# Sharing one buffer between the cosine's argument and g, a fourth P buffer, normalisation per tile, unchecked registers and a new order in a sparse-attention and cosine-MLP kernel

## The chip, the cores and the metric

One Trainium2 chip, one of its cores. The metric is the device time of one execution in microseconds (us); the smaller the better. Engines are TensorE (PE; its weight loads are shown as PEld), VectorE (DVE), ScalarE (ACT), GpSimd (POOL) and SyncE (SP, which only issues DMAs here). A q behind an engine's name means its sequencer.

## What is computed

Block-sparse attention over 4 batches of 8 heads, 768 positions and 64 dimensions, then a feed-forward layer whose nonlinearity is h cos(h):

```python
mask = |block_i - block_j| <= 1, or block_i or block_j first or last   # blocks of 32
mask |= three sampled blocks for each query block
attn = softmax(where(mask, q @ k.T / 8, -1e9))
x = (attn @ v)            # (4, 8, 768, 64) -> (3072, 512)
h = x @ w_in              # w_in is 512 x 2048, float64
out = (h * cos(h)) @ w_out   # w_out is 2048 x 512, float64
```

## The kernel before

**Tiles.** The 3072 rows are 24 query tiles of 128 rows, six to a batch. Five of the six are sparse: each row of queries sees 11 blocks of keys (352 columns). The sixth holds the first and the last blocks and is dense (768 columns, as 2 x 384). A sparse tile is worked in four units of two heads, a dense one in eight units of one head. Two tiles make one feed-forward m of 256 rows; there are 12 of them. A feed-forward has four pieces p of 512 hidden columns.

**Precision.** Operands are split into a high and a low half of float16; a product is high x high, high x low and low x high. V is stored as [high | low], 128 columns a head.

**A unit.** Scores into the PSUM tile `sp` (one slot), bias add with maximum into `P` (`mx`), a small op for the exponent's bias (`nb`), exp (`ex`, its row sums go to `sums`), high half into `ring` (`ph`, ScalarE), low half (`pl`, VectorE), a DMA transpose of `ring` to `PT`, then the products with V into the PSUM tile `xp` (`pv`). `P`, `ring` and `PT` have three slots each.

**Values.** In `sparse_values` (L1641, L1653) and `dense_values` (L1666) a wide unit multiplies the high half of P by [V high | V low], 128 columns, and the low half by V high, 64 columns, so that `xp` has 128 columns a head for four heads, one PSUM bank. Sparse tiles before number 6 are `thin`: three products of 64 columns that add up in the same 64 columns. A sparse unit has first its quarter products (96 x 32 weights at four row positions), then its full ones.

**Normalisation** comes after two sparse or four dense units, twice a tile (`normalize`): offset of the sums (`rs`, L1679 or L1682), reciprocal (`rr`, L1686), multiply by it (`no`, L1689), for wide tiles an add of the two 64-column halves (`xa`, L1691), cast to float16 (`xh`, L1693) and the rest (`xl`, L1696), all on VectorE. The DMA transpose to `xT` follows once a tile is complete.

**A feed-forward piece.** TensorE makes 48 "up" matmuls (L1831) into `ph`; ScalarE evacuates them to `hs` (L1840, two slots) in two halves; VectorE rounds (`round_a`, `round_b`, L1845 and L1848) into `kt` (one slot); ScalarE takes the sine in place (L1851, another table than exp's); VectorE multiplies back into `hs` (L1855); ScalarE and VectorE write the high and low halves of `g` (L1861 and L1864, four slots); TensorE makes 24 "down" matmuls (L1873).

**Start.** The first k and v are loaded and scaled; a scale comes from a Gram product on TensorE (L1316), a reduction (L1319) and a spread. 32 weight blocks arrive as float64, are converted by integer operations on VectorE (L1742 to L1746), scaled and split. Raw blocks lie in weight tiles that are not yet in use and, for the last eight, in `g` slots. The third v load lies in the `kt` slot. Sampled indices are loaded into registers (`load_regs`, L1204) on VectorE and ScalarE, eight and four for each of five tile positions, with a check of each value against its bounds.

**Order.** No engine's order is written out. Each operation has an engine, a cost, a position in time (from `PARAMS` and a nudge by its name from `NUDGES`), its operands and its slots. `Plan.run` is a list scheduler that goes through all engines at once, takes on each the runnable operation of least position, and hands out slots in the sequence of the first operations' positions. What results is a fixed program order for each engine; on the chip the engines run in order and wait for one another by semaphores. The lines that put the rounding where it is:

```python
op("DVE", 0.602, pos + ae(p, 2) + pr["KT"], lambda hs=hs, kt=kt: e.round_a(hs.t, kt.t), r=[hs], w=[kt], name=f"ka{m}_{p}")
op("ACT", 0.947, pos + ae(p, 5) + pr["GH"], lambda hs=hs, g=g: e.g_hi(hs.t, g.t), r=[hs], w=[(g, 0)], name=f"gh{m}_{p}")
```

with KT = -33.478 and GH = 9.373.

Of the kernel before, what the change touches and what calls it, by code (L numbers as in the profile page):

```python
# [13 lines left out]
F32 = mybir.dt.float32  # L14
I32 = mybir.dt.int32
AF = mybir.ActivationFunctionType
ALU = mybir.AluOpType
# [3 lines left out]
P = 128  # L21
BLK = 32
# [13 lines left out]
    VLEAD=6.432, EVAC=-1.668, KT=-33.478, SN=-2.897, GM=-10.655, GH=9.373, GL=8.736, TSTICK=31.117,  # L36
# [6 lines left out]
    RG=[0.0, -3.58, 20.03, 0.0, -2.44], RA=[2.07, 9.34, 0.26, 1.6, 9.28], PV3=[1, 1, 1, 1, 1, 1],  # L43
# [4 lines left out]
    QLP=[0, 0, 0, 0, 0, 0], XLP=[0, 0, 0, 0, 0, 0],  # L48
# [9 lines left out]
    idx=-7.77, sx=31.62, regs=-0.29, regs0=4.25, regs0_0=0.33, regs1=15.75, regs1_0=-22.8, regs2=48.02, regs2_0=5.02, regs0_1=-18.23, const=25.72,  # L58
    kload=-0.12, kload0=3.07, kload0_0=-4.36, ksq=1.03, ksq0=0.62, ksq0_0=-19.66, kload0_1=-3.8, ksq0_1=4.89, kload0_2=-15.73, ksq0_2=-6.31,
    kred=-16.28, kred0=11.53, kall=-0.88, kall0=-3.2, ksc=-8.35, ksc0=-5.35, regs3=3.42, regs3_0=9.11, regs4=-9.54, regs4_0=0.87, regs2_1=-7.41,  # L60
    regs3_1=5.19, regs4_1=1.21, vload=1.17, vload0=-0.48, vload0_0=1.69, vsq=1.1, vsq0=-8.19, vsq0_0=3.52, vload0_1=-1.23, vsq0_1=1.21,
    vload0_2=28.21, vsq0_2=-20.52, vred=17.47, vall=0.47, vall0=-18.65, vsc=7.33, vsc0=0.49, ql=-1.59, ql0=-2.36, qsq=0.12, qsq0=-0.63, qsc=-0.5,
    qsc0=-28.56, qu=-1.19, qu0=-3.51, qnu=3.74, qnu0=-8.16, qhi=1.19, qhi0=-7.92, qlo=0.44, qlo0=11.7, uT=-0.15, uT0=14.1, up=-12.11, up0=-4.28,
    khi=4.28, khi0=8.38, klo=4.06, klo0=6.12, kT=2.7, kT0=-7.25, kT0_2=0.33, kp=-2.83, kp0=3.56, kp0_2=-1.28, kT0_3=-12.7, kp0_3=10.63, kT0_4=3.23,
    kp0_4=3.3, kT0_5=1.89, kp0_5=5.32, vhi=0.77, vhi0=-1.22, vhi0_0=-11.14, vlo=-20.9, vlo0=-1.23, vlo0_0=5.58, vst=13.41, vst0=1.18, vst0_0=-16.89,
    vhi0_1=0.55, vlo0_1=-4.78, vhi0_2=-11.3, vlo0_2=-10.17, vst0_2=10.69, vhi0_3=14.56, vlo0_3=10.79, vst0_3=-18.61, vhi0_4=0.71, vlo0_4=23.48,
    vst0_4=7.73, vhi0_5=3.61, vlo0_5=-14.89, vst0_5=1.21, vg=-0.55, vg0=34.29, vg0_0=34.43, vg0_1=6.76, vg0_2=-25.78, vi=8.02, vi0=-3.57, vi0_0=7.48,
    vi0_1=-3, vi0_2=8.01, vi0_3=-37.84, wgd=-1.11, wgd0=-17.02, wga=0.34, wga0=13.21, wl=-6.98, wl0=1.07, wc=0.23, wc0=-0.77, wc0_0=-7.39,
    wc0_2=-6.83, wsq=-9.45, wsq0=13.98, wl1=1.26, wc1=11.01, wc1_0=-3, wc1_1=4.52, wc1_2=-3.38, wsq1=5.06, wl2=-11.17, wl3=4.27, wc3=-1.76,
# [1882 lines left out]
```

## Time and profile before

| | |
|---|---|
| three runs | 868.88, 874.35, 879.92 us, median 874.35 |
| profiled execution | 885.61 us, its span 883.8 us |
| PE busy, its mean granted clock | 739.3 us (84%), 0.94 |
| DVE busy | 681.3 us (77%) |
| ACT busy | 628.2 us (71%) |
| POOL busy | 99.4 us (11%) |
| DMA | 146.45 MB, mean 166 GB/s |

The times are of separate executions; the profile is of another one, and its durations fit its own time. Busy time of an engine leaves out its register and semaphore work. An engine that is busy 80% of a span may still not be what ends last, which is why the stretches and the chain of waits are read beside it.

### The profile page before, as it was taken

The page shows a single profiled execution, that of the slowest core. Times are in us where ns is not written, and L with a number is a line of the kernel's source. Part 1 is how long each engine was busy: PE and PEld are TensorE (multiplying, and loading weights), DVE is VectorE, ACT ScalarE, POOL GpSimd, SP SyncE. Part 2 cuts the span into 40 slices and gives each one's busy share as a digit, 9 for nine tenths or more (in the row PEclk, how much of TensorE's full clock was granted, in tenths as well). Part 3 has the DMA queues.
Part 4 walks back from the last instruction along what each step waited for, and adds up shares of the span by engine and source line. Part 5 has one row for each costly group of instructions (what it writes and reads, how often), then busy time and mean ns, then how long its engine had stood idle before and what let it go on. Part 6 is the DMA issues. An engine that isn't in the chain of part 4 may idle for free.

```text
span 883.8 us, 21557 instructions
## 1 busy us (share of the span) xinstructions
PE 739.3 (84%) x8360; PEld 506.6 (57%) x8360; DVE 681.3 (77%) x1813; ACT 628.2 (71%) x1181; POOL 99.4 (11%) x128
## 2 busy tenths in 40 slices
PE   2445687769698898999999888989999789899997
PEld 2334564457456556758566457657675458467583
DVE  1868999998966887878867975989868768866652
ACT  1655765889766987767867976779669847959442
POOL 5021220000021021200022021200040111000000
PEclk9997688869989999999999889999999789999999
DMA  8799894587886999794778998794888997963400
GB/s 253 239 245 209 214 234 133 130 173 149 168 226 149 172 217 176 145 212 91 139 230 168 188 190 186 150 216 84 187 198 148 180 168 151 215 107 76 82 7 24
DMA packets 316118, 146.45 MB, mean 166 GB/s; under 512 B 266480, under 2 KB 291184, under 8 KB 316016
## 3 DMA queue, kind: packets, MB, share of 16 engines
q1 hardware_dynamic: 310896, 129.35, 70.8%
q0 software_dynamic: 5120, 15.73, 7.8%
q8 instruction: 65, 1.06, 0.5%
q14 instruction: 37, 0.30, 0.1%
HBM read 68.23 MB, written 12.58 MB: 91 GB/s over the span
## 4 chain that ended last, share of the span: by engine, by line
PE 36%; DVE 25%; DMA 17%; ACT 10%; issue 6%; DVEq 2%; another core or an unknown queue 2%; SPq 1%; ACTq 0%
PE po L1873 14%; PE ph L1831 14%; DMA PT<-ring 7%; DVE P L1580 4%; DVE ring L1616 2%; DMA W<-kn 2%; DMA stage<-in_k_dram 2%; ACT P L1602 2%; PE xp L1653 2%; DVE hs L1855 2%; DVEq L1204 2%; PE sp L1564 2%; DVE kt L1848 2%; DMA w<-in_moe_w_out_dram 2%
## 5 line engine op out<-in xcount | busy, mean ns | idle before, releaser
L1873 PE MATMUL po<-w,g 128*128 128x512 f16 x1152 | 285.3, 397 | 12.5 <-DVE kn L1889 5.8
L1831 PE MATMUL ph<-xT,w 128*128 128x256 f16 x2304 | 266.0, 274 | 11.7 <-DMA xT<-n 4.3
L1831 PEld LDWEIGHTS <-w 128*128 128x128 f16 x2304 | 224.3, 98 | 48.6 <-issue 11.3
L1873 PEld LDWEIGHTS <-g 128*128 128x128 f16 x1152 | 110.2, 101 | 139.6 <-issue 29.4
L1602 ACT ACTIVATE P<-P,sm 128x352 f32<-128x352 f32 (+1 forms) x224 | 152.1, 680 | 51.4 <-DVE sm L1597 45.4
L1519 POOL DMA_INDIRECT V<-scr,gidx x80 | 88.1, 1101 | 646.6 <-PE xp L1641 288.5
L1616 DVE TENSOR_TENSOR ring<-P,ring 128x704 f16<-128x704 f32 (+1 forms) x112 | 100.3, 905 | 16.5 <-ACT ring L1612 16.2
L1580 DVE CUSTOM_DVE_ANT_1 P<-sp,bias 128x352 f32<-128x352 f32 x160 | 78.5, 518 | 29.8 <-PE sp L1553 15.6
L1840 ACT ACTIVATE hs<-ph,sm 128x512 f32<-128x512 f32 x96 | 64.1, 678 | 44.6 <-PE ph L1831 30.5
L1612 ACT CAST ring<-P 128x704 f16<-128x704 f32 (+1 forms) x112 | 86.6, 785 | 10.4 <-DMA PT<-ring 9.6
L1547 PE MATMUL sp<-W,U 128*128 128x192 f16 x320 | 54.8, 272 | 39.8 <-DVE sm L1580 31.5
L1855 DVE SCALAR_TENSOR_TENSOR hs<-hs,sm,kt 128x1024 f32<-128x1024 f32 x48 | 61.5, 1280 | 18.8 <-ACT kt L1851 18.5
L1851 ACT ACTIVATE kt<-kt,sm 128x1024 f32<-128x1024 f32 x48 | 55.1, 1147 | 22.2 <-DVE kt L1848 22.0
L1861 ACT ACTIVATE g<-hs 128x1024 f16<-128x1024 f32 x48 | 50.1, 1049 | 27.2 <-DVE hs L1855 27.2
L1864 DVE TENSOR_TENSOR g<-hs,g 128x1024 f16<-128x1024 f32 x48 | 58.3, 1219 | 6.3 <-ACT g L1861 5.7
L1548 PEld LDWEIGHTS <-U 128*128 128x128 f16 x320 | 33.7, 105 | 48.4 <-issue 44.9
L1848 DVE SCALAR_TENSOR_TENSOR kt<-kt,hs 128x1024 f32<-128x1024 f32 x48 | 58.6, 1220 | 0.4
L1845 DVE TENSOR_SCALAR kt<-hs 128x1024 f32<-128x1024 f32 x48 | 33.1, 690 | 30.3 <-ACT hs L1840 29.6
L1548 PE MATMUL sp<-W,U 128*128 128x64 f16 x320 | 50.1, 210 | 2.4 <-DMA W<-kn 2.2
L1653 PE MATMUL xp<-V,PT 128*128 128x128 f16 (+1 forms) x720 | 46.5, 214 | 3.5 <-issue 3.5
L1641 PE MATMUL xp<-V,PT 96*32 96x64 f16 (+1 forms) x1440 | 31.6, 215 | 20.4 <-DMA PT<-ring 18.8
L1602 ACT ACTIVATION_READ_ACCUMULATOR P<-P,sm 128x1 f32 x224 | 42.0, 188 | 0.0
(176 smaller groups left out, 930.7 us busy)
## 6 DMA issues: line engine op xcount, KB each, us to landing
V<-scr SPq DMA_DIRECT2D x20, 384.0 KB
stage<-in_k_dram SPq DMA_DIRECT2D x12, 512.0 KB
w<-in_moe_w_in_dram SPq DMA_DIRECT2D x12, 512.0 KB
w<-in_moe_w_out_dram SPq DMA_DIRECT2D x12, 512.0 KB
V<-scr SPq DMA_DIRECT2D x24, 256.0 KB
scr<-n SPq DMA_DIRECT2D x21, 256.0 KB
qs<-in_q_dram SPq DMA_DIRECT2D x20, 256.0 KB
U<-U SPq DMA_DIRECT2D x40, 128.0 KB
```

The source lines that it names most:

```text
L1519: self.nc.gpsimd.indirect_dma_start(V[:96, 2 + j, :], None, self.scr[b][:, :], bass.IndirectOffsetOnAxis(ap=self.gidx[:96, c : c + 1], axi ...
L1548: mm(spv[:, :, 96:128].rearrange("p y (n c) -> p y n c", c=hf), u, ends, start=False, stop=False)
L1580: self.nc.vector.tensor_tensor_reduce(out=self.p_view(n, Pt)[:, a].rearrange("p (n c) -> p n c", c=hf), in0=sp[:, :w].rearrange("p (n c) - ...
L1602: self.nc.scalar.activation(Pv[:, a], Pv[:, a], AF.Exp, scale=qc[:, 4:5], bias=nb[:, bcol : bcol + 1], accum_out=sums[:, 2 * kk + a : 2 * ...
L1612: self.nc.scalar.copy(R[:, :, 0, : self.width(n)], self.p_view(n, Pt))
L1616: self.nc.vector.tensor_tensor(R[:, :, 1, :w], self.p_view(n, Pt), R[:, :, 0, :w], ALU.subtract)
L1653: mm(xp[:, hl, : d1 - d0], PT[:, 6 * a + 3 * l + c, :], V[:, c, h, d0:d1], start=False, stop=(a == 1 and c == 1 and x == len(terms) - 1),)
L1831: self.nc.tensor.matmul(ph[:, ff, :], self.W1[p][:, wl, cc, c * P : (c + 1) * P], xT[:, xl * NCC + cc, :], start=(j == 0), stop=(j == len( ...
L1840: self.nc.scalar.activation(hs[:, h * 512 : h * 512 + 512], ph.rearrange("p f t -> p (f t)"), AF.Copy, scale=self.turns[b][:, p : p + 1])
L1848: self.nc.vector.scalar_tensor_tensor(kt, kt, MAGIC, hs, op0=ALU.subtract, op1=ALU.subtract)
L1855: self.nc.vector.scalar_tensor_tensor(hs, hs, c[:, p : p + 1], kt, op0=ALU.mult, op1=ALU.mult)
L1873: self.nc.tensor.matmul(po, g[:, gl, ff, t * P : (t + 1) * P], self.W2[p][:, wl, ff, :], start=(first and ff == half * hf and j == 0), sto ...
```

## The change

- `kt` goes. The argument of the cosine lies, as float32, in the `g` slot whose halves it becomes: `round_a`, `round_b`, `cosine` and `g_mul` take g and view it as float32. A g slot is so taken by `round_a` and no longer by the high half. The third v load of the start lies in a `g` slot.
- `P` has four slots.
- Every tile is thin: three products of 64 columns a head in all units, `xp` holds eight heads of 64 columns. Normalisation comes once a tile on 512 columns, without the add; the cast to float16 goes to ScalarE. `sums` and `rs` get twice the width and half the slots.
- Sampled indices are clamped to 0..23 by VectorE ahead of the multiply, and the register loads are told to skip their bounds checks.
- The position of the rounding is `ae(p, 5) + KT` with KT = 9.373, equal to that of the high half of g. Some costs of the planner change (DMA_DONE 0.94 to 1.15, TABLE_LOAD 1.283 to 1.41, MODE_SWITCH 0.13 to 0.10, a gather's DMA 0.87 to 1.5, the sparse scores 0.83 to 0.78, register loads and two constants). Of the nudges, 2575 of the 2582 that both versions have get other values, 414 go and 136 are new. All other positions in `PARAMS` stay.

```diff
-    SHIFT=..., KT=-33.478, ...
+    SHIFT=..., KT=9.373, ...
...
-            vst[b] = [Val("hs"), Val("hs"), Val("kt")]
+            vst[b] = [Val("hs"), Val("hs"), Val("g")]
...
+        rs, y = Val("rs"), Val("ot")
+        np_ = vpos + at(7) + pr["NORM"]
+        f = lambda x: e.normalize(x, n, sums.t, xp.t, rs.t, y.t, xn.t)
+        op("DVE", 0.08, np_ - 1.5, lambda: f(0), r=[sums], w=[rs], name=f"rs{n}")
+        op("DVE", 0.1, np_ - 1.5, lambda: f(1), w=[rs], name=f"rr{n}")
+        op("DVE", 0.602, np_, lambda: f(2), r=[rs, xp], w=[y], name=f"no{n}")
+        op("ACT", 0.525, np_ + 0.01, lambda: f(3), r=[y], w=[(xn, 0)], name=f"xh{n}")
+        op("DVE", 0.602, np_ + 0.01, lambda: f(4), r=[y, (xn, 0)], w=[(xn, 1)], name=f"xl{n}")
...
-            op("DVE", 0.602, pos + ae(p, 2) + pr["KT"], lambda hs=hs, kt=kt: e.round_a(hs.t, kt.t), r=[hs], w=[kt], name=f"ka{m}_{p}")
+            op("DVE", 0.602, pos + ae(p, 5) + pr["KT"], lambda hs=hs, g=g: e.round_a(hs.t, g.t), r=[hs], w=[g], name=f"ka{m}_{p}")
...
-        stage=[None] * 3, hs=[None] * 2, kt=[None], g=[None] * 4, kn=[None] * 2, n16=[None] * 3,
-        qs=[None], U=[None] * 2, P=[None] * 3, ring=[None] * 3, PT=[None] * 3, V=[None] * 2,
+        stage=[None] * 3, hs=[None] * 2, g=[None] * 4, kn=[None] * 2, n16=[None] * 3,
+        qs=[None], U=[None] * 2, P=[None] * 4, ring=[None] * 3, PT=[None] * 3, V=[None] * 2,
...
-        s["xp"] = slots("xp", n["xp"], [P, 4, 2 * D], F32, psum)
+        s["xp"] = slots("xp", n["xp"], [P, H, D], F32, psum)
...
-            self.sx, sidx.rearrange("p (b t) -> p b t", t=2)[:, :, 0], BLK // 2, None, op0=ALU.mult
+            self.sx, sidx.rearrange("p (b t) -> p b t", t=2)[:, :, 0], 0, NB - 1, op0=ALU.max, op1=ALU.min
         )
+        nc.vector.tensor_scalar(self.sx, self.sx, BLK // 2, None, op0=ALU.mult)
...
+            skip_runtime_bounds_check_because="the indices were clamped to the blocks that there are",
...
-        terms = [(0, 0, D), (0, D, 2 * D), (1, 0, D)] if thin else [(0, 0, 2 * D), (1, 0, D)]
+        terms = [(0, 0, D), (0, D, 2 * D), (1, 0, D)]
...
-            w = D if thin else 2 * D
-            nc.vector.tensor_tensor(y[:, :, :w], xp[:, :, :w], rs.unsqueeze(2).to_broadcast([P, 4, w]), ALU.mult)
+            nc.vector.tensor_tensor(y, xp, rs.unsqueeze(2).to_broadcast([P, H, D]), ALU.mult)
         elif x == 3:
-            nc.vector.tensor_tensor(y[:, :, 0:D], y[:, :, 0:D], y[:, :, D : 2 * D], ALU.add)
-        elif x == 4:
-            nc.vector.tensor_copy(xn[:, 0, hg], y[:, :, 0:D])
+            nc.scalar.copy(xn[:, 0], y)
         else:
-            eng = nc.gpsimd if x == 6 else nc.vector
-            eng.tensor_tensor(xn[:, 1, hg], y[:, :, 0:D], xn[:, 0, hg], ALU.subtract)
+            nc.vector.tensor_tensor(xn[:, 1], y, xn[:, 0], ALU.subtract)
...
-    def round_a(self, hs, kt):
+    def f32(self, t):
+
+        return t if t.dtype == F32 else t.bitcast(F32)
+
+    def round_a(self, hs, g):
+        kt = self.f32(g)
         self.nc.vector.tensor_scalar(kt, hs, 0.25, MAGIC, op0=ALU.add, op1=ALU.add)
```

## Rows read from the trace of the kernel before

**Rows 1.** Busy time of each engine by stretch, with clock and DMA share

```profile
0.00:60.00 60.00, 21.67 (x235) 17.60 (x237) 31.77 (x101) 21.75 (x40) 19.12 (x56) 1.00 0.87 246
60.00:200.00 140.00, 96.26 (x1440) 71.51 (x1435) 133.70 (x358) 103.27 (x196) 13.73 (x12) 0.79 0.77 186
200.00:780.00 580.00, 522.05 (x5901) 351.03 (x5900) 460.74 (x1263) 448.68 (x871) 66.53 (x60) 0.96 0.88 172
780.00:884.00 104.00, 99.34 (x794) 66.49 (x792) 55.08 (x93) 54.56 (x76) 0.00 (x0) 1.00 0.28 56
```

The columns are: stretch, length, busy time (and instructions) of PE, PEld, DVE, ACT and POOL, granted clock of PE, DMA share, GB/s.

**Rows 2.** The chain that ended last, shares of the span by engine

```profile
PE 36%; DVE 25%; DMA 17%; ACT 10%; issue 6%; DVEq 2%; another core or an unknown queue 2%; SPq 1%; ACTq 0%
```

**Rows 3.** Line 1204, the register loads: ns min/median/max, first and last start

```profile
L1204 DVEq FUSED_REGOPS  x40: 183/183/206, 8.3 to 51.4; - x40
L1204 DVEq SEQ_ASSERT  x40: 23/23/41, 8.6 to 51.6; - x40
```

**Rows 4.** Timeline of the start: start us, us, what, idle time before

```profile
10.56 1.89 PE L1316 MATMUL ph<-stage 128*128 128x128 bf16 x16 [0.72 <-DMA stage<-in_k_dram]
...
19.30 0.29 DVE L1319 TENSOR_REDUCE sm<-ph 128x1 bf16<-128x128 f32 x1 [12.44 <-issue]
```

**Rows 5.** Timeline of TensorE: a thin sparse, a wide sparse, a dense unit

```profile
130.47 0.36 PE L1641 MATMUL xp<-V,PT 96*32 96x64 f16 x24 [1.50 <-DMA PT<-ring]
130.77 0.52 PE L1653 MATMUL xp<-V,PT 128*128 128x64 f16 x12
131.13 1.48 PE L1831 MATMUL ph<-xT,w 128*128 128x256 f16 x12
...
337.82 0.35 PE L1641 MATMUL xp<-V,PT 96*32 96x128 f16 x16
...
338.45 1.46 PE L1873 MATMUL po<-w,g 128*128 128x512 f16 x6
...
222.22 0.67 PE L1666 MATMUL xp<-V,PT 128*128 128x128 f16 x12
222.73 1.46 PE L1873 MATMUL po<-w,g 128*128 128x512 f16 x6
```

**Rows 6.** Groups by line and shape: busy us, mean ns, idle time before

```profile
L1689 DVE TENSOR_TENSOR ot<-xp,sm 128x512 f32<-128x512 f32 (+1 forms) x48 | 30.1, 628 | 5.8 <-PE xp L1653 2.2 <-PE xp L1666 2.1 <-DMA out_dram<-ot 1.3
L1691 DVE TENSOR_TENSOR ot<-ot 128x256 f32<-128x256 f32 x38 | 16.0, 421 | 0.3
L1693 DVE CAST n<-ot 128x256 f16<-128x256 f32 x48 | 13.8, 288 | 2.8 <-DMA scr<-n 2.5
L1696 DVE TENSOR_TENSOR n<-ot,n 128x256 f16<-128x256 f32 x48 | 20.1, 420 | 0.4
L1686 DVE RECIPROCAL sm<-sm 128x4 f32<-128x4 f32 x48 | 7.2, 167 | 0.2
...
L1612 ACT CAST ring<-P 128x704 f16<-128x704 f32 x80 | 60.5, 769 | 4.2 <-DMA PT<-ring 3.6
L1616 DVE TENSOR_TENSOR ring<-P,ring 128x704 f16<-128x704 f32 x80 | 70.1, 886 | 7.9 <-ACT ring L1612 7.8
L1653 PEld LDWEIGHTS <-PT 128*128 128x128 f16 x720 | 34.1, 104 | 10.5 <-issue 4.0
```

**Rows 7.** Timeline of two feed-forward pieces of the fourth feed-forward

```profile
360.32 1.15 ACT L1851 ACTIVATE kt<-kt,sm 128x1024 f32<-128x1024 f32 x1 [1.07 <-DVE kt L1848]
...
360.39 1.21 DVE L1864 TENSOR_TENSOR g<-hs,g 128x1024 f16<-128x1024 f32 x1
...
361.98 1.24 ACT L1840 ACTIVATE hs<-ph,sm 128x512 f32<-128x512 f32 x2
```

**Rows 8.** Waits: who waited for whom, us in total, times, longest

```profile
ACT kt L1851 <- DVE kt L1848: 22.0, 19, 2.2
```

**Rows 9.** Timeline: a rounding, and the last downs of four pieces before

```profile
281.18 0.69 DVE L1845 TENSOR_SCALAR kt<-hs 128x1024 f32<-128x1024 f32 x1
...
284.45 1.46 PE L1873 MATMUL po<-w,g 128*128 128x512 f16 x6
```

More of the change, by code (lines that the diff above doesn't have):

```diff
@@ L604, in load_regs @@
         x = pr["XD"][i]
-        eng, cost, p = (("DVE", 0.25 + 0.275 * x, pr["RG"][i]), ("ACT", 0.25 + 0.275 * (12 - x), pr["RA"][i]))[which]
+        eng, cost, p = (("DVE", 0.05 + 0.236 * x, pr["RG"][i]), ("ACT", 0.05 + 0.236 * (12 - x), pr["RA"][i]))[which]
         op(eng, cost, p, lambda: e.load_regs(i, which), r=[(tmp, "sx")], w=[regs[i, which]], name=f"regs{i}_{which}", after=after)
@@ L782, in attend @@
         nu = 4 if sparse else 8
-        hg_n = nu // 2
-        thin = sparse and n < 6 and pr["PV3"][n]
         xn = Val("n16")
@@ L1012, in plan_kernel @@
     ib = [(tmp, "a"), (tmp, "smp")]
-    op("POOL", 7.9, pr["CB"], lambda: e.const_b(tmp.t), r=ib, w=[(bias, 1), (tmp, "b")], name="const_b", after=[by["kall0"]])
+    op("POOL", 7.6, pr["CB"], lambda: e.const_b(tmp.t), r=ib, w=[(bias, 1), (tmp, "b")], name="const_b", after=[by["kall0"]])
     for which in range(2):
@@ L1018, in plan_kernel @@
     ic = [(tmp, "a"), (tmp, "smp")]
-    op("POOL", 8.4, pr["CC"], lambda: e.const_c(tmp.t), r=ic, w=[dbias, (tmp, "b")], name="const_c", after=[o for o in pl.ops if o.name == "vall0"])
+    op("POOL", 5.7, pr["CC"], lambda: e.const_c(tmp.t), r=ic, w=[dbias, (tmp, "b")], name="const_c", after=[o for o in pl.ops if o.name == "vall0"])
     prep_q(0, pr["Q0"])
@@ L1118, in __init__ @@
         s["hs"] = slots("hs", n["hs"], [P, 1024], F32)
-        s["kt"] = slots("kt", n["kt"], [P, 1024], F32)
         s["g"] = slots("g", n["g"], [P, 2 * self.FP * TK], F16)
@@ L1842, in up_out, with round_b, cosine, g_mul @@
         )
-    def round_a(self, hs, kt):
+    def f32(self, t):
+        return t if t.dtype == F32 else t.bitcast(F32)
+    def round_a(self, hs, g):
+        kt = self.f32(g)
         self.nc.vector.tensor_scalar(kt, hs, 0.25, MAGIC, op0=ALU.add, op1=ALU.add)
-    def round_b(self, hs, kt):
+    def round_b(self, hs, g):
+        kt = self.f32(g)
         self.nc.vector.scalar_tensor_tensor(kt, kt, MAGIC, hs, op0=ALU.subtract, op1=ALU.subtract)
-    def cosine(self, kt):
+    def cosine(self, g):
+        kt = self.f32(g)
         self.nc.scalar.activation(kt, kt, AF.Sin, scale=-SIN_SCALE, bias=self.halfpi)
-    def g_mul(self, b, p, early, hs, kt):
+    def g_mul(self, b, p, early, hs, g):
+        kt = self.f32(g)
         c = self.cge if early else self.cg[b]
```

606 lines of the change are left out of this document (285 added, 321 removed).

## The prediction

> **What bounds the kernel now.** I read the table of stretches first [rows 1]. It shows three stages. In the first 60 us TensorE works a third of the time and VectorE half, while the DMA engines are 87% busy: keys, values and the first weights come in. From 60 to 200 us VectorE is busy 133.7 of 140 us (95%): it converts the weights from float64 while the first tiles already run. From 200 to 780 us TensorE is busy 522 of 580 us, with VectorE at 79% and ScalarE at 77%; its granted clock is 0.96, so a few stretches run at the lower level. After 780 us TensorE is busy 99 of 104 us: the rest of the last feed-forward, all matmul. So work taken from TensorE counts nearly in full, work taken from VectorE counts in full only up to 200 us, and afterwards only where TensorE waits: 58 us idle, and 0.04 x 580 = 23 us lost to the lower clock. Second view, the chain that ended last, by engine [rows 2]: VectorE holds 25% of it, ScalarE 10%, DMA 17%. I use those shares as prices for work whose place in the chain I can't follow.
>
> **The register checks, at the start.** VectorE's queue runs five loads of eight registers, and after each load eight pairs of a range test (183 ns) and an assert (23 ns), 40 pairs in all: 8 x 0.206 = 1.65 us a load [rows 3]. Three loads stand ahead of the reduction that gives the scale of k. Its matmuls end at 10.56 + 1.89 = 12.45 us, the reduction starts at 19.30, and VectorE idled 12.44 us before it, from 6.86 [rows 4]: 4.15 us for each load. Without checks three loads take 12.44 - 3 x 1.65 = 7.5 us, so the reduction can start at 14.4 instead of 19.3: 4.9 us earlier. The other two loads stand between works of VectorE, 2 x 1.65 = 3.3 us. That is 8.2 us. The clamp adds one small VectorE operation, some 0.2 us by the reciprocal's 167 ns [rows 6]. Everything else in the first stage starts from those scales, but the weights' DMAs can hide part: the DMA engines had 0.13 x 60 = 7.8 us to spare there [rows 1]. I take 6 us, from 2 to 8.2. ScalarE's 20 checks lie where it was idle: nothing.
>
> **Normalisation per tile.** Now it comes twice a tile, on half the heads each. All of it by the groups [rows 6]: 30.1 (multiply) + 16.0 (add of the two halves of a product) + 13.8 (cast) + 20.1 (subtract) + 7.2 (reciprocal), and about 7.2 again for the small operation ahead of it, are 94.4 us of VectorE in 48 halves. After: per tile a multiply and a subtract of 512 columns, which I read between the 256-column subtract (420 ns) and the 704-column one of the rings (886 ns) as 690 ns each, and two small ones of 167 ns: 1.71 us, times 24 = 41 us. Gone are 53 us of busy time. Small operations overlap their neighbours by about 80 ns, which the row means count twice: there are 278 before and 96 after, so 182 x 0.08 = 15 us of that is not queue time, and 38 us remain. Where do they lie? The four tiles normalised before 200 us are already of the narrow kind: a multiply of 256 columns (as the subtract, 420), cast, subtract and two small ones, 2 x (420 + 288 + 420 + 167 + 167) = 2.9 against 1.7 us, less six overlaps of 0.08, is 0.7 us each: 3 us on a busy VectorE, all of it on the path. The other 35 us lie beside TensorE. At the chain's 25% they give 9 us; the ends are 0 (all hidden) and 35 (VectorE the pacemaker throughout).
>
> The cast moves to ScalarE: 24 x 610 ns (769 ns for 704 columns [rows 6], scaled) = 14.6 us, at ScalarE's 10% of the chain 1.5 us, from 0 to 14.6. It also makes one hop more, VectorE, ScalarE, VectorE, ahead of the transpose to xT; xT feeds ups that TensorE runs when it has nothing better, and the last tile's xT is needed long before the end.
>
> **Values with 64 columns.** For tiles from the sixth on, and the dense ones, a product of 128 columns becomes two of 64 on the same weights, loaded twice. The trace has both kinds at the full clock [rows 5]. Narrow: from 130.47 to 131.13, 0.66 us a unit. Wide: 337.82 to 338.45, 0.63. Dense and wide: 222.22 to 222.73, 0.51 for 12 matmuls. The narrow unit is made of 24 quarter products and 12 full ones; its 12 full ones take 131.13 - 130.77 = 0.36, 30 ns each, so a dense unit of 18 would take 0.54. Sum: 60 x 0.03 + 32 x 0.03 = 2.8 us of TensorE, counted in full. [...]
>
> **One buffer for argument and halves.** kt had a single slot, so the rounding of a piece waited for the multiply of the piece before. Now the argument lies in one of the four g slots. This frees the rounding from the multiply: at 360.32 the second sine waited 1.07 us for its rounding [rows 7], which could have been done beside the first sine. Two hs slots still allow only two pieces at once. Over the run such waits of ScalarE come to 22.0 us in 19 places [rows 8]; at 10% of the chain 2 us, from 0 to 10. What it adds: a g slot is now held from the rounding on, not from the first half on, and it comes free only when the downs of the piece four before are done. I compared the 44 pieces: 43 rounded after those downs, mostly by 5 to 60 us. In one the rounding started at 281.18, while the last downs of that slot ran from 284.45 for 1.46 us [rows 9]: some 4.7 us once. During the weights' load the same slots hold raw weights, and the third v load now needs one too; the first conversions free them in time. I take 0, up to 8 us of loss.
>
> **Fourth P buffer, planner constants, new order.** P is held from the bias add to the subtract of the ring; a fourth slot can only start exps earlier, and rings and PT stay at three. Nothing, or a few us of gain. The position of the rounding moves from 33 us ahead of its piece to 9 us behind, equal to that of the first half, so that slots are taken in the same sequence. Nearly all nudges change too. The order decides how the 58 idle us of the middle stage are filled; I can't read it off a diff, and take 0 with 15 us to either side.
>
> **Sum.** -6 (checks) - 3 (early normalisation) - 9 (late normalisation) + 1.5 (cast) + 2.8 (matmuls) - 2 (argument) = -15.7 us. The profiled execution took 885.6 us, with a span of 883.8; the median of three runs is 874.35, 1.3% lower. On the median: 858.7, say 859 us, 1.8% less.
>
> **Rivals.** *VectorE is the pacemaker of the middle stage too.* For it: many short waits of ScalarE end with VectorE. Against: TensorE at 90%. Then the late normalisation counts at some 80%, 28 us instead of 9, and the time is 840. *TensorE hides all but the start.* Then -6 - 3 + 2.8 = -6.2, 868 us, and with a poorer order some us more. For it: the last 100 us and much of the middle are pure matmul. *Slower, through hs.* The rounding's place in the order now lies behind the attention work on VectorE. An hs slot is held from its evacuation to the last half, and there are two. At 361.98 the evacuation for the third piece started right when the last half of the first ended, 360.39 + 1.21 = 361.60 [rows 7]: in such bursts hs already sets the pace of the ups. If the rounding then sits behind one attention unit on VectorE (two bias adds, a small one, a ring subtract of 0.89 [rows 6]; about 2 us), two pieces of each of 11 feed-forwards come 2 us late, 44 us of ups. It decides where more than half of that meets an idle TensorE: 25 us lost against 16 won, 884 us, and with a bad order up to 900. Against it: TensorE mostly has downs in store. [...] If each extra full load cost the 104 ns its row shows [rows 6], 60 x 4 + 32 x 6 = 432 loads add 45 us: 904. The 30 ns steps of rows 5 all but exclude it. [...] *The edit does not do what it says:* the range tests could stay in the queue in another form; then 6 us less gain, 865.
>
> **Chances and range.** Forecast and its surroundings, 850 to 866: 0.41. Only the start is won, 866 to 880: 0.22, and 0.04 for checks that stay. VectorE paces, 830 to 850: 0.20. Slower through hs or the order, 880 to 900: 0.11. Weight loads: 0.02. To hold 8 in 10 the range leaves out the lowest 0.09 and the highest 0.11: 835 to 882. A measurement of this kernel tells about 2% from no change, that is 857 and 892: faster 0.20 + 0.20 of the forecast's 0.41, 0.40; slower 0.06 (a half of the third rival, and the weight loads); within, 0.54.
>
> **What would show each step.** In the first 25 us the reduction of k should start near 14.4 with no range tests in VectorE's queue. Late groups: 24 multiplies, 24 subtracts of about 690 ns, VectorE near 628 us busy, ScalarE near 643. A narrow unit of values at 0.66 us, a dense one at 0.54, and TensorE busy about as now. Rounding steps that start before the multiply ahead of them. The middle stage's idle time of TensorE is the judge: below 50 us I was right, at 58 the second rival, above 70 the third. The prediction is wrong if the start does not shift, or if evacuations wait for the last half of g more than the bursts of now.

## The result, and the profile after

| | before | after |
|---|---|---|
| median of 17 runs each, us | 878.81 (868.83 to 886.15) | 866.14 (861.08 to 872.37) |
| profiled execution, us (span) | 885.61 (883.8) | 865.76 (863.6) |

The ratio is 0.9899, 95% interval 0.9865 to 0.9933: 1.0% faster, some 9 us. The medians in the table are of all runs, while the ratios, here and below, leave out runs more than 1.5% above the fastest of their kernel, here three of before. Forecast were 15.7 us, 1.8%. The two profiled executions differ by 20 us, twice the ratio's share: that of before had 17.8 us of stalls of TensorE, which come in some sets of runs only (last section).

The stretches of the kernel after, in the columns of [rows 1]:

```profile
0.00:60.00 60.00, 28.18 (x415) 22.64 (x416) 43.33 (x145) 32.55 (x64) 21.34 (x56) 0.70 0.98 262
60.00:200.00 140.00, 101.28 (x1370) 73.44 (x1369) 128.18 (x311) 100.92 (x187) 22.31 (x12) 0.75 0.73 183
200.00:780.00 580.00, 531.26 (x6880) 367.49 (x6878) 433.53 (x1122) 455.07 (x887) 64.75 (x60) 0.96 0.88 172
```

More work is done in the first 60 us: VectorE 43.3 us for 31.8, TensorE 28.2 for 21.7. From 200 to 780 us VectorE has 27 us less to do and TensorE is idle 48.7 us instead of 58, yet the chain of waits hardly changed [rows 2]:

```profile
PE 35%; DVE 22%; DMA 20%; ACT 12%; issue 6%; SPq 2%; DVEq 1%; ACTq 0%
```

The start [rows 4], with no range tests left in VectorE's queue:

```profile
12.61 0.29 DVE L1289 TENSOR_REDUCE sm<-ph 128x1 bf16<-128x128 f32 x1 [5.41 <-PE ph L1286]
...
16.02 1.45 DVE L1275 SCALAR_TENSOR_TENSOR kn<-stage,sm,kn 128x512 f16<-128x512 f32 x2 [1.86 <-ACT kn L1272]
```

The reduction starts at 12.61 us, 6.7 us earlier than before and 1.8 earlier than forecast, and what ends its wait is now the matmul ahead of it. The value units [rows 5], timeline of TensorE:

```profile
201.35 0.36 PE L1611 MATMUL xp<-V,PT 96*32 96x64 f16 x24
201.64 0.52 PE L1623 MATMUL xp<-V,PT 128*128 128x64 f16 x12
202.00 1.47 PE L1798 MATMUL ph<-xT,w 128*128 128x256 f16 x12
...
217.60 0.69 PE L1637 MATMUL xp<-V,PT 128*128 128x64 f16 x18
218.12 2.75 PE L1848 MATMUL po<-w,g 128*128 128x512 f16 x12
```

From a unit's first start to the start of what follows: 0.65 us sparse, 0.52 dense, against 0.63 and 0.51 in the wide form. Of 47 roundings, 10 now start before the multiply of the piece ahead; before it was none. Normalisation and cast, groups by line [rows 6], and in a fence of its own the wait that stood in [rows 8]:

```profile
L1663 DVE TENSOR_TENSOR n<-ot,n 128x512 f16<-128x512 f32 x24 | 16.3, 688 | 2.9 <-ACT n L1661 2.9
L1659 DVE TENSOR_TENSOR ot<-xp,sm 128x512 f32<-128x512 f32 x24 | 16.3, 687 | 7.5 <-PE xp L1623 3.8 <-PE xp L1637 3.5
L1661 ACT CAST n<-ot 128x512 f16<-128x512 f32 x24 | 14.5, 611 | 12.6 <-DVE ot L1659 11.3 <-DMA scr<-n 1.2
```

```profile
ACT g L1825 <- DVE g L1821: 16.8, 10, 2.8
```

ScalarE got these 14.5 us of casts, and yet was busy 629.8 us, 1.6 more than before and not the 643 of the forecast's signs: the new order switches its tables 39 times for 47 (1283 ns each), which saves 10.3 us.

### The profile page after: what moved, and what is told of

Same layout as the page of the kernel before. It is cut to its first block, busy times and chain, and to the rows that moved or that the text cites. A ratio compares the mean times of both kernels' runs of the same rounds, so it can differ in the third digit from the quotient of the medians.

```text
span 863.6 us, 23056 instructions
## 1 busy us (share of the span) xinstructions
PE 739.9 (86%) x9272; PEld 513.7 (59%) x9272; DVE 645.9 (75%) x1632; ACT 629.8 (73%) x1197; POOL 108.4 (13%) x128
## 4 chain that ended last, share of the span: by engine, by line
PE 35%; DVE 22%; DMA 20%; ACT 12%; issue 6%; SPq 2%; DVEq 1%; ACTq 0%
PE ph L1798 18%; PE po L1848 10%; DMA PT<-ring 9%; DMA xT<-n 5%; DVE P L1550 3%; ACT P L1572 3%; DVE hs L1830 2%; DVE ring L1586 2%; DVE g L1821 2%; DMA stage<-in_k_dram 2%; ACT ring L1582 2%; ACT hs L1807 1%; DMA W<-kn 1%; DVE g L1839 1%; DVE w L1275 1%
## 5 line engine op out<-in xcount | busy, mean ns | idle before, releaser
L1798 PE MATMUL ph<-xT,w 128*128 128x256 f16 x2304 | 279.2, 281 | 21.4 <-DMA xT<-n 9.8
L1848 PE MATMUL po<-w,g 128*128 128x512 f16 x1152 | 271.7, 385 | 2.0 <-DVE g L1839 1.3
L1489 POOL DMA_INDIRECT V<-scr,gidx x80 | 96.1, 1201 | 619.6 <-PE xp L1611 295.5
L1550 DVE CUSTOM_DVE_ANT_1 P<-sp,bias 128x352 f32<-128x352 f32 x160 | 77.9, 520 | 17.2 <-PE sp L1523 16.8
L1830 DVE SCALAR_TENSOR_TENSOR hs<-hs,sm,g 128x1024 f32<-128x1024 f32 x48 | 61.1, 1282 | 19.2 <-ACT g L1825 18.9
L1825 ACT ACTIVATE g<-g,sm 128x1024 f32<-128x1024 f32 x48 | 54.7, 1145 | 17.2 <-DVE g L1821 16.8
L1836 ACT ACTIVATE g<-hs 128x1024 f16<-128x1024 f32 x48 | 50.4, 1050 | 16.8 <-DVE hs L1830 16.3
L1817 DVE TENSOR_SCALAR g<-hs 128x1024 f32<-128x1024 f32 x48 | 33.0, 689 | 36.2 <-ACT hs L1807 32.6
L1821 DVE SCALAR_TENSOR_TENSOR g<-g,hs 128x1024 f32<-128x1024 f32 x48 | 58.6, 1222 | 0.8
L1611 PE MATMUL xp<-V,PT 96*32 96x64 f16 x1920 | 32.2, 205 | 28.8 <-DMA PT<-ring 26.8
L1611 PEld LDWEIGHTS <-PT 96*32 96x32 f16 x1920 | 22.1, 103 | 44.9 <-DMA PT<-ring 33.7
L1623 PE MATMUL xp<-V,PT 128*128 128x64 f16 x960 | 47.6, 205 | 0.0
```

Source lines behind the costliest of these rows:

```text
L1489: self.nc.gpsimd.indirect_dma_start(V[:96, 2 + j, :], None, self.scr[b][:, :], bass.IndirectOffsetOnAxis(ap=self.gidx[:96, c : c + 1], axi ...
L1550: self.nc.vector.tensor_tensor_reduce(out=self.p_view(n, Pt)[:, a].rearrange("p (n c) -> p n c", c=hf), in0=sp[:, :w].rearrange("p (n c) - ...
L1798: self.nc.tensor.matmul(ph[:, ff, :], self.W1[p][:, wl, cc, c * P : (c + 1) * P], xT[:, xl * NCC + cc, :], start=(j == 0), stop=(j == len( ...
L1821: self.nc.vector.scalar_tensor_tensor(kt, kt, MAGIC, hs, op0=ALU.subtract, op1=ALU.subtract)
L1830: self.nc.vector.scalar_tensor_tensor(hs, hs, c[:, p : p + 1], kt, op0=ALU.mult, op1=ALU.mult)
L1848: self.nc.tensor.matmul(po, g[:, gl, ff, t * P : (t + 1) * P], self.W2[p][:, wl, ff, :], start=(first and ff == half * hf and j == 0), sto ...
```

## The experiments

Five sets of runs, each beside runs of the kernel before. In sets 1 (before at 878.7 us) and 3 (879.1) no wait of TensorE in the profiles of the changed kernels ends in "issue", that is in nothing the profile shows. In sets 2 (889.6), 4 (890.8) and 5 (883.9) such waits sum to 9 to 26 us a profile; sets 1 and 2 ran on the same chip. Differences are taken inside a set.

**Checks back in the kernel after** (set 1):

```diff
-            skip_runtime_bounds_check_because="the indices were clamped to the blocks that there are",
+            bass_reorder=True,
```

> The changed kernel with the bounds checks of the register loads put back, every engine's order as it is; the clamp stays. My theory: the start waits 5 us longer for the scale of k and the whole kernel some 6 us longer than the changed one, a ratio to the kernel before near 0.997. Rival, the start is hidden by the DMA engines: no loss, a ratio near 0.990. Rival, the checks are nearly all of the gain: at or above 1.000.

Measured: 878.74 us, ratio 1.000 (0.9965 to 1.0035). The line put in is not in before, but VectorE's queue shows the same 40 range tests as there. The first stretch (table of stretches) is near that of before again, and so is the reduction's start (timeline of VectorE):

```profile
0.00:60.00 60.00, 20.69 (x243) 16.96 (x244) 33.50 (x109) 22.74 (x41) 20.06 (x56) 0.95 0.79 227
```

```profile
19.50 0.29 DVE L1289 TENSOR_REDUCE sm<-ph 128x1 bf16<-128x128 f32 x1 [12.44 <-issue]
```

In the new order the checks are worth the whole gain of 1.0%, with half a per cent to either side; the forecast's 0.997 lies within the interval too.

**Checks off in the kernel before** (set 1):

```diff
-            self.sx, sidx.rearrange("p (b t) -> p b t", t=2)[:, :, 0], BLK // 2, None, op0=ALU.mult
-        )
+            self.sx, sidx.rearrange("p (b t) -> p b t", t=2)[:, :, 0], 0, NB - 1, op0=ALU.max, op1=ALU.min
+        ); nc.vector.tensor_scalar(self.sx, self.sx, BLK // 2, None, op0=ALU.mult)
...
+            max_val=(self.S - BLK) // 2, skip_runtime_bounds_check_because="the indices were clamped to the blocks that there are",
```

> The kernel before with clamped indices and no bounds checks, every engine's order as it was. My theory: 6 us less, a ratio of 0.993. Hidden by DMA: 1.000. The checks are the whole gain: 0.990.

Measured: 871.52 us, ratio 0.9925 (0.9888 to 0.9961), 6.6 us less. The first stretch, and the start in the timeline of VectorE:

```profile
0.00:60.00 60.00, 25.99 (x311) 20.66 (x311) 40.12 (x131) 28.82 (x54) 19.20 (x56) 0.67 1.03 272
```

```profile
12.43 0.29 DVE L1319 TENSOR_REDUCE sm<-ph 128x1 bf16<-128x128 f32 x1 [5.34 <-PE ph L1316]
```

So the checks' term, -6, holds. All other parts, the order with them, take the kernel from 0.9925 to 0.9899, a ratio of 0.9974; the two half intervals, 0.37 and 0.34%, make 0.5% together. That is -2.3 us, from -7 to +2. Forecast for them were -15.7 + 6 = -9.7. The stretch from 200 to 780 us shows how little TensorE got of the 35 to 38 us less that VectorE has to do there, this run first, the kernel after of set 3 below it:

```profile
200.00:780.00 580.00, 528.00 (x6009) 359.43 (x6007) 468.98 (x1287) 453.74 (x879) 67.33 (x60) 0.97 0.89 173
200.00:780.00 580.00, 528.39 (x6826) 365.61 (x6824) 431.40 (x1120) 452.15 (x879) 65.15 (x60) 0.96 0.89 172
```

TensorE's idle time is 52.0 us here and 51.6 there, 48.7 in the first profile of after; from 200 us to the end it is 56.5, 56.0 and 53.1, and TensorE is busy 606.8, 610.9 and 610.5 us. These are single profiles, and this run's was 6 us faster than its median.

**The kernel after with the nudges of before** (set 1): the dictionary `NUDGES` of before in place of its own.

> All edits of the change, but the nudges of the kernel before, so that the planner makes another order of the new work. My theory has the order worth nothing on average: near 0.990. Rival, the edits win more and the new order gives some back: below 0.985. Rival, the order is what wins: 1.000 or above.

Measured: 906.99 us, ratio 1.0359 (1.0307 to 1.0412). From 400 to 600 us, this run first and the kernel after below it:

```profile
400.00:600.00 200.00, 169.74 (x2199) 116.52 (x2198) 142.14 (x372) 152.08 (x298) 20.87 (x20) 0.92 0.90 167
```

```profile
400.00:600.00 200.00, 189.94 (x2427) 135.06 (x2425) 155.50 (x383) 164.30 (x315) 21.80 (x20) 0.98 0.89 174
```

TensorE is 20 us less busy in the same 200 us: the order, not the amount of work. Whether the edits upset it, or any order without nudges of its own would be as bad, needed the next two.

**The kernel before with the planner's costs of after, nothing else** (set 3):

```diff
-        eng, cost, p = (("DVE", 0.25 + 0.275 * x, pr["RG"][i]), ("ACT", 0.25 + 0.275 * (12 - x), pr["RA"][i]))[which]
+        eng, cost, p = (("DVE", 0.05 + 0.236 * x, pr["RG"][i]), ("ACT", 0.05 + 0.236 * (12 - x), pr["RA"][i]))[which]
...
-                op("POOL", 1.03, ipos + 0.8 + j * 0.5, lambda j=j: e.v_gather(n, V.t, j), r=[scr[b], gidx], w=[(V, 10 + j)], dma=0.87, name=f"vi{n}_{j}")
+                op("POOL", 1.03, ipos + 0.8 + j * 0.5, lambda j=j: e.v_gather(n, V.t, j), r=[scr[b], gidx], w=[(V, 10 + j)], dma=1.5, name=f"vi{n}_{j}")
...
```

> The kernel before with nothing but the planner's costs of the kernel after (register loads, gathers, sparse scores, two constants), so that the same instructions come in another order: TensorE's and VectorE's queues differ in most rows, GpSimd's not at all. If the nudges are fitted to the costs, and any order that they were not searched for is some per cent worse, 890 to 915 for a before of 880, ratio 1.01 to 1.04, as the old nudges under the new code gave 1.036. If it was the edits that upset the order in that run, no difference here beyond 0.5%.

Measured: 927.68 us, ratio 1.055 (1.0493 to 1.0606). (The diff leaves out three more costs: sparse scores 0.83 to 0.78, two constants 7.9 to 7.6 and 8.4 to 5.7.) The same instructions in another order end further above the kernel before than the changed kernel did with the old nudges. From 200 to 780 us TensorE was busy 504.0 us, 18 less than before. The first theory holds, with a loss larger than its 1.01 to 1.04: nudges fit one set of costs.

**The kernel after with three P buffers** (set 3):

```diff
-        qs=[None], U=[None] * 2, P=[None] * 4, ring=[None] * 3, PT=[None] * 3, V=[None] * 2,
+        qs=[None], U=[None] * 2, P=[None] * 3, ring=[None] * 3, PT=[None] * 3, V=[None] * 2,
```

> The kernel after with three P buffers for four and its own nudges; the planner then makes another order (VectorE's and TensorE's queues differ in most rows). If the fourth buffer carries some of the gain, exps wait for the ring's subtract, and the time is 1% or more above the kernel after with waits of ScalarE's exps on P. If only a searched order is what is lost, the loss is of the same size as in the run with the costs alone, and no such waits show. Within 0.5% of the kernel after: neither matters here.

Measured: 925.65 us, ratio 1.0521 (1.0477 to 1.0565), 56 us above the kernel after in this set, a loss of the size of the last. No wait of an exp on a buffer shows; but the order switches ScalarE's tables more often, groups by line of this run and of the kernel after in the same set:

```profile
L1825 ACT ACT_TABLE_LOAD x28 | 35.9, 1283 | 0.5
L1572 ACT ACT_TABLE_LOAD x27 | 34.6, 1283 | 2.1 <-DVE sm L1564 1.6
```

```profile
L1825 ACT ACT_TABLE_LOAD x20 | 25.7, 1283 | 2.7 <-DVE g L1821 2.4
L1572 ACT ACT_TABLE_LOAD x19 | 24.4, 1283 | 0.3
```

16 loads more are 20.5 us of ScalarE. Before had 24 and 23. The two runs above had only 2 loads more than after and 4 more than before, so switches are not what every such order loses by. What the fourth buffer is worth with nudges made for three wasn't tried.

**The cast back on VectorE** (set 1):

```diff
-            nc.scalar.copy(xn[:, 0], y)
+            nc.vector.tensor_copy(xn[:, 0], y)
```

> The changed kernel with the cast of the normalised rows on VectorE instead of ScalarE, at the same places of the order. 24 casts of about 0.53 us go to VectorE, 12.7 us, and 14.5 us leave ScalarE. My theory (VectorE counts for 25% past the start, ScalarE for 10%): 1.5 to 2 us slower than the changed kernel, within its noise, 0.992. Rival, VectorE paces the middle stage: 10 us slower, 1.001. Rival, TensorE hides both: 0.990.

Measured: 865.86 us, ratio 0.9875 (0.9824 to 0.9925), not to be told from the kernel after. VectorE is busy 6.6 us more, not 12.7, and ScalarE 12.5 less.

**Less work for VectorE, in the order of before** (set 2):

```diff
-            w = D if thin else 2 * D
+            w = D
...
-            nc.vector.tensor_tensor(y[:, :, 0:D], y[:, :, 0:D], y[:, :, D : 2 * D], ALU.add)
+            nc.vector.tensor_copy(y[:, :, 0:1], y[:, :, 0:1])
```

> The kernel before, with its checks and its order of instructions on every engine, and less work for VectorE: the multiply of the 38 wide halves takes 256 columns for 512 (684 ns each before, 415 ns for the narrow ones: 38 x 0.27 = 10.2 us), and the add of 256 columns (421 ns) becomes a copy of one column (some 0.1 us: 38 x 0.32 = 12.2 us). The output lacks the product of the high half of P with the low half of V in these tiles. In all some 22 us of VectorE's busy time go, mostly after 200 us; TensorE's work stays. Theory of the forecast, a quarter of it is on the path: -5.5 us, ratio 0.994. Theory 'TensorE hides it': no difference, 1.000. Theory 'VectorE is the pacemaker': -18 us or more, 0.980 or less.

Measured: 885.61 us, ratio 0.9961 (0.9928 to 0.9994). VectorE is busy 663.2 us, 18 less, and by the ratio 3.5 us come back, 19%, with 0.5 to 6.4 us in the interval.

**The same with 64-column products** (set 2):

```diff
-        terms = [(0, 0, D), (0, D, 2 * D), (1, 0, D)] if thin else [(0, 0, 2 * D), (1, 0, D)]
+        terms = [(0, 0, D), (0, D, 2 * D), (1, 0, D)]
...
-            for l, w in ((0, 2 * D), (1, D)):
+            for x, (l, d0, d1) in enumerate([(0, 0, D), (0, D, 2 * D), (1, 0, D)]):
```

> The run with less work for VectorE in the order of before, and the products of values in 64 columns in every tile, so that the output is whole: 40 wide units and 32 dense ones have three products of 64 columns for one of 128 and one of 64, on weights loaded once more (some 430 full loads more); the order of everything else is as before. Against the run without them: by the forecast's term, 0.03 us a unit, +2.2 us, ratio 0.9965 if the smaller VectorE work is worth a quarter; if matmuls there are covered by TensorE's idle time, no difference between the two; if each added load cost the 104 ns of its row, +45 us, 1.045.

Measured: 895.22 us, ratio 1.006 (1.0027 to 1.0093): by the ratios 8.8 us above the run without the split, 4 to either side. The split adds 912 matmuls (12 in each of 60 wide units, 6 in each of 32 dense ones). None of the three theories gave that cost.

**More work for VectorE in the kernel after** (set 2):

```diff
-            nc.vector.tensor_tensor(y, xp, rs.unsqueeze(2).to_broadcast([P, H, D]), ALU.mult)
+            for _ in range(2): nc.vector.tensor_tensor(y, xp, rs.unsqueeze(2).to_broadcast([P, H, D]), ALU.mult)
...
-            nc.vector.tensor_tensor(xn[:, 1], y, xn[:, 0], ALU.subtract)
+            for _ in range(2): nc.vector.tensor_tensor(xn[:, 1], y, xn[:, 0], ALU.subtract)
```

> The kernel after, in its order, with the multiply and the subtract of each tile's normalisation issued twice (the second writes the same again): 48 instructions of 687 ns, 33 us more of VectorE, all but some 5 us of it after 200 us. The mirror of the term that failed: if a quarter of VectorE's work lies on the path, +8 us over after, 874, ratio 0.995 to before; if TensorE hides it, as after, 866 and 0.987 to 0.990; if VectorE paces, +28 us, 894 and 1.018.

Measured: 894.8 us, ratio 1.0074 (1.0043 to 1.0106), VectorE busy 676.3 us. There was no kernel after beside it in this set.

**The third product left out of the kernel after** (set 2, and set 3 beside the kernel after):

```diff
-        terms = [(0, 0, D), (0, D, 2 * D), (1, 0, D)]
+        terms = [(0, 0, D), (0, D, 2 * D)]
```

> The kernel after, in its order, without the third product (low half of P with the high half of V) in every unit: 1152 matmuls and their weight loads go of 3456, by the rows of after a third of 47.6 + 32.2 + 22.5 = 102.3 us, 34 us of TensorE; VectorE, ScalarE and all transfers work as before. The output lacks that product. If TensorE's own work sets the time, -34 us less what waits take its place: between -34 and -17 us from 866, 832 to 849, ratio 0.947 to 0.967. If waits for transfers and VectorE set it as much, -8 us or less, 858 and 0.977 or more.

> The kernel after, unchanged, as the point of comparison on the chip that runs the others of this call, since the kernel before took 889.6 us in the runs of the last four and 878.7 in those ahead of them. If the change is worth the same share there, ratio 0.990 to before (0.9865 to 0.993). [...]

> The kernel after without the third product of values, for the comparison with the kernel after on one chip. Theory 'TensorE's own work sets the time': the 13 to 34 us of TensorE that go come back at least by half, 0.985 or less of the kernel after. Theory 'TensorE is one of several, its value products wait for P's transposes and fill gaps that stay': 0.995 to 1.000 of it.

Measured: 0.9871 (0.9822 to 0.992) in set 2. In set 3 the kernel after took 869.2 us, ratio 0.9887 (0.9848 to 0.9925), which repeats the result, and without the product 858.66 us, 0.9767 (0.9716 to 0.9819). Its units are shorter by a third, timeline of TensorE:

```profile
200.07 0.30 PE L1611 MATMUL xp<-V,PT 96*32 96x64 f16 x16
200.30 0.41 PE L1623 MATMUL xp<-V,PT 128*128 128x64 f16 x8
200.54 1.47 PE L1798 MATMUL ph<-xT,w 128*128 128x256 f16 x12
```

0.47 us for 0.65. TensorE's busy time falls by 18.4 us, from 739.1 to 720.7, and 10.5 us come back: 57%. The gain lies between the two theories; the forecast had counted TensorE's time in full.

**The split and VectorE's work again, with the kernel after beside them** (set 4): the same edits.

> The kernel before with less work for VectorE in its own order (18 us less by the profile of its first run; the output lacks the product of the high half of P with the low half of V in the wide tiles), on a chip without the stalls of TensorE if it is another. A quarter of it on the path: -4.5 us, ratio 0.995. Hidden by TensorE: 1.000. VectorE the pacemaker: -14 us or more, 0.984 or less. On the first chip it was 0.996.

> The same with the products of values in 64 columns, 912 matmuls more than the run beside it. By the forecast's term +2.8 us over that run, ratio 0.998 if that one is 0.995. By the price of a matmul in the run without the third product (10.5 us for 1152) +8.3 us, ratio 1.005. On the first chip the difference was 9.6 us, 4 of them in stalls.

> The kernel after with the multiply and the subtract of each tile issued twice, 30 us more of VectorE by the profile of its first run. A quarter of it on the path: +7.6 us over the kernel after beside it, ratio 0.998 to before if after is 0.9895. Hidden: no difference. VectorE the pacemaker: +24 us or more, 1.017.

> The kernel after, unchanged, beside the run with more work for VectorE: 0.990 to the kernel before as in two sets of runs; nearer to 1.000 if the chip is the one with the stalls of TensorE and those take back the gain.

Measured: 888.33 us (0.9962, 0.9931 to 0.9994), 897.56 (1.0085, 1.0051 to 1.012), 900.21 (1.0078, 1.0034 to 1.0122), and the kernel after 891.99, ratio 1.0003 (0.9966 to 1.0039). By the ratios the split costs 10.9 us, 4 to either side. 31 us more of VectorE cost 6.7 us over the kernel after, 21%, with 5 to either side; 18 us less give 3.4 us, 19%. And in this set the change itself is worth nothing, with 0.4% to either side.

**A third time** (set 5), the split with less of VectorE, and more of VectorE:

> The kernel before in its order with the narrow multiply, without the adds, and with value products of 64 columns, for the third time. In a set without stalls: a median unit grew from 0.64 to 0.65 us and the dense units by 0.2 to 0.3 us in all, so the split costs 1 to 2 us, and with 18 us less of VectorE at a quarter (-4.5 us) the ratio is 0.997; with VectorE's work hidden, 1.002; if the split costs 9 us there too, 1.005 or more. In a stalled set again 1.006 to 1.0085.

> The kernel after with 31 us more of VectorE, for the third time. In a set without stalls the kernel after stands at 0.989 to 0.990: with a quarter of the added work on the path 0.998, with all of it hidden 0.990, with half of it 1.007. In a stalled set again 1.0075.

Measured: 894.77 us (1.0124, 1.0086 to 1.0162) and 894.74 us (1.0115, 1.0078 to 1.0151). The set had stalls again, so what the two terms are without them stays open. Neither the kernel after nor the run with less of VectorE alone was in this set, so no term can be taken from it.

## Why the forecast was right in direction and too large

**Which step failed.** The checks' term held, and the shortfall lies in the parts behind it: forecast at -9.7 us, they brought -2.3 (-7 to +2) by the run without checks in the old order, and nothing by the run with checks in the new one. Two of their terms were tried alone, both in sets with stalls. There the late normalisation had the price that the forecast gave it, within wide intervals, and the 64-column products cost three to four times their +2.8. In the sets without stalls, where the forecast was missed, neither was tried alone, and which of the two fell short there stays open.

**Register checks, -6: right.** 6.6 us in the order of before. Of its working, the start moved 6.7 us, not 4.9: the reduction no longer waits for the loads at all, but for its matmul.

**Late normalisation, -9 by a quarter of 35 us: the price held where it could be measured.** VectorE's busy time fell by 35.4 us, 681.3 to 645.9, against 38 forecast (the sign "near 628" takes off 53 and leaves out the overlaps; the working gives 643). By the ratios its price was 19% both times that work was taken away in the old order, and 21% when it was added in the new one, all in sets with stalls and with intervals from a few per cent to over a third. VectorE is no pacemaker; the first rival falls. The second, that TensorE hides all but the start, falls only in those sets. Its 868 us is nearest to what came, and in the sets without stalls TensorE's idle time from 200 us on fell by 0.5 to 3 us only, not by 9, with 36 us less of VectorE there. That speaks against this term there, but the order changed with it, and it is three profiles.

**Values with 64 columns, +2.8: too small by three to four times where it was tried.** The step took the cost from undisturbed units, 0.03 us each. Those grew by 0.01 to 0.02 us as said. But 912 more matmuls, with their loads, cost 8.8 and 10.9 us in the sets with stalls. The cause is not shown. TensorE was busy 8.4 and 5.3 us longer by the profiles, while its waits for nothing that shows went from 20.9 to 25.0 us in set 2 and from 25.5 to 16.8 in set 4; longer stalls are thus not the common cause. At about 9 us the sum would be -15.7 + 6.6 = -9.1, near the measured 9, but that puts a price from sets with stalls, where the change gained nothing, into sets without them. There only the other direction was measured, 1152 matmuls less for 10.5 us, which is 8.3 us for 912; but those took columns of V away, which the split does not add. TensorE's busy time from 200 us on grew by about 4 us there (606.8 to 610.9 and 610.5), nearer to the forecast. The rival by which each added full load costs the 104 ns of its row, 45 us in all, falls: 8.8 to 10.9 us over 912 are 10 to 12 ns for each added load and matmul, or, all put on the 432 full loads among them, 20 to 25 ns for each.

**Early normalisation -3, argument -2, cast +1.5.** The cast's place made no difference that the interval could show. Waits of the sine on its argument fell from 22.0 to 16.8 us. Neither this nor the early part was tried by itself.

**Order, 0 with 15 to either side: too narrow a view of it.** Without nudges of their own three kernels came out 4.6% (the kernel after with the old ones: ratios 1.036 over 0.990), 5.5% (before with other costs: 927.7 over 879.1) and 6.5% (three P buffers: 925.7 over 869.2) above the kernel that they were made from. Every edit that makes the planner choose again is therefore mixed with a new search, and the difference between two searched orders is part of the -2.3 that all parts but the checks brought. How much of it is order can't be told: no run has the new nudges on the old code.

**Slower through hs.** Waits of ups on the evacuation were 6.4 us after and 3.4 before, one of 4.8 us among them; no 25 us were lost.

**The judge.** TensorE's idle time from 200 to 780 us fell to 48.7, below the 50 that was to prove the forecast, and yet over a third of the gain was missing. Its 58 came from a profile of before with stalls in it: without them the kernel before with its checks off had 52.0. A stretch with fixed ends also holds other work once the start has moved.

## What to carry to other kernels

Where a planner orders the instructions, try an edit with the order held fixed; one that re-plans measures the search, here 4.6 to 6.5% of it against edits of 1%. A share of the chain of waits was a usable price for VectorE's time (a quarter, measured about a fifth, in sets with stalls only), while matmuls added there cost several times their length in an undisturbed stretch (8.8 and 10.9 us, for 2.8 by the rows). A price holds for the set of runs that it was measured in. Checks on registers ahead of the first scale held the start up by 6.9 us in the order of before, and the whole kernel by 6.6.

## What was not expected of the hardware

**Stalls with nothing to wait for.** In three of five sets TensorE stood still in stretches of some 3 us, most of them while GpSimd issued a tile's gathers (19 of the 20 such waits in the profile of before touch an issue or lie within 0.4 us of one): one or two matmuls every 0.7 to 1.4 us. Timeline of the run with less work for VectorE in set 4, TensorE, then GpSimd, then VectorE:

```profile
337.55 0.26 PE L1653 MATMUL xp<-V,PT 128*128 128x128 f16 x2
338.43 0.24 PE L1653 MATMUL xp<-V,PT 128*128 128x128 f16 x2 [0.62 <-issue]
339.86 0.24 PE L1653 MATMUL xp<-V,PT 128*128 128x128 f16 x2 [1.19 <-issue]
340.57 0.23 PE L1653 MATMUL xp<-V,PT 128*128 128x128 f16 x1 [0.47 <-issue]
341.31 0.23 PE L1653 MATMUL xp<-V,PT 128*128 128x64 f16 x1 [0.51 <-issue]
...
335.25 0.92 POOL L1519 DMA_INDIRECT V<-scr,gidx  x1 [14.53 <-PE xp L1641]
336.48 1.00 POOL L1519 DMA_INDIRECT V<-scr,gidx  x1 [0.30 <-issue]
337.78 0.92 POOL L1519 DMA_INDIRECT V<-scr,gidx  x1 [0.30 <-issue]
339.00 0.92 POOL L1519 DMA_INDIRECT V<-scr,gidx  x1 [0.30 <-issue]
...
341.39 0.52 DVE L1580 CUSTOM_DVE_ANT_1 P<-sp,bias 128x352 f32<-128x352 f32 x1 [3.33 <-remote]
```

TensorE's waits were 25.5 us in that run, 16.8 us in the one with the split beside it, 17.8 us in the profiled execution of before and none in that of after. The kernel after in set 4, whose gain was gone, had 16.9 us of them.

VectorE and ScalarE stood still as well. In every profile of sets 2, 4 and 5, and in that of before, VectorE's bias adds waited 9 to 22 us in all for a releaser that the profile only calls "remote"; no profile of sets 1 and 3, nor that of after, has such a wait. The kernel after in set 4, TensorE, VectorE and ScalarE:

```profile
721.63 0.35 PE L1523 MATMUL sp<-Wg,U 128*32 128x96 f16 x16
...
726.66 0.53 DVE L1550 CUSTOM_DVE_ANT_1 P<-sp,bias 128x352 f32<-128x352 f32 x1 [5.08 <-remote]
...
726.74 0.69 ACT L1867 ACTIVATE ot<-po,sm 128x512 f32<-128x512 f32 x1 [3.88 <-remote]
```

The bias add came 4.7 us after the end of the scores that it reads, and GpSimd had issued gathers from 720.69 to 725.29. TensorE then waited for VectorE, so what a stall costs is more than TensorE's waits for nothing.

The start was hit too. The bias add there, set 4 first and set 3 below, then the first stretch of both in the same order:

```profile
48.97 0.53 DVE L1550 CUSTOM_DVE_ANT_1 P<-sp,bias 128x352 f32<-128x352 f32 x1 [5.17 <-issue]
```

```profile
43.34 0.53 DVE L1550 CUSTOM_DVE_ANT_1 P<-sp,bias 128x352 f32<-128x352 f32 x1 [0.50 <-PE sp L1523]
```

```profile
0.00:60.00 60.00, 23.26 (x271) 18.58 (x272) 38.54 (x126) 27.58 (x51) 22.45 (x56) 0.70 0.85 240
0.00:60.00 60.00, 28.74 (x403) 23.03 (x407) 42.95 (x145) 32.56 (x64) 20.38 (x56) 1.00 0.94 261
```

So 4.4 us of VectorE's work came later in set 4. All profiles go the same way: without checks VectorE is busy 42.6 to 43.4 us of the first 60 in kernels made from after in sets 1 and 3, and 37.3 to 39.3 in sets 2, 4 and 5; with checks 33.1 and 33.5 without stalls, 31.8 to 32.6 with them. The stalls thus take more from the early start than from the late one, and the checks' 6.6 us were measured only in a set without stalls. How much of the change's gain set 4 lost at the start, and how much by the split, was not tried. What makes a set stall was not found; the chip alone is not it, since sets 1 and 2 shared one.
